# One decode step of attention with a gated block on one core: the gate moved to the start, one TensorE loop for all pairs, products moved to VectorE

## The chip, the core and the metric

The kernel runs on one core of a Trainium2 chip. The metric is the device time of one execution in microseconds. The kernel before took 687.77 us (median of three runs, 687.76 to 687.81). Lower is better.

## What is computed

```python
def reference(A_x, A_k_cache, A_v_cache, A_wq, A_wo, B_x, B_w_gate, B_w_up, B_w_down):
    x = A_x                                    # [1, 1, 512]
    xn = layernorm(x)                          # without scale and shift
    q = xn @ A_wq                              # 512 x 4096: 32 heads of 128
    scores = q . k_cache * 128 ** -0.5         # caches: 32 heads x 8192 x 128, float32
    o = softmax(scores) . v_cache
    s = o.reshape(4096) @ A_wo                 # 4096 x 512
    h = sigmoid(xn @ w_gate) * (xn @ w_up)     # 512 x 1376 each
    g = silu(h @ w_down)                       # 1376 x 512
    return x + s * g
```

Everything is float32. The two caches hold 134 MB each, wq and wo 8.4 MB each, the three matrices of the gated block 2.8 MB each: each byte is read once.

## The kernel before

The 32 heads are taken as 16 **pairs**. A pair's keys are one transfer of 64 KB to each of the 128 partitions, that is 8.389 MB: 64 partitions for a head, 128 positions of 128 numbers in each. Its values are another one. SBUF holds three such **slots**: keys of even and odd pairs alternate between slots 0 and 1, slot 2 holds values. All loads of consequence are issued by SP (SyncE) into one queue, in the order in which SP's program names them; SP stands still at a wait, and what it issues behind the wait comes later.

Work of pair i:

- VectorE (`scores`, L279 to L284): the whole key block times the query in place (L281), a sum over each position's 128 products (L282), and each partition's maximum (L284). With its last sum done, the slot is free for the keys of pair i+2.
- TensorE (`pair`, L244 to L262), a loop with the waits on semaphores written out: turns the maxima into a row (L246), VectorE takes the maximum of each head (`all_max`, L276), TensorE spreads it over the partitions (L248), ScalarE makes the exponentials with their sums (`powers_of`, L294 and L296), TensorE adds the sums (L250) and multiplies weights and values (L255, 32 groups of two instructions, into `po`). Then slot 2 is free for the next values. ScalarE copies `po` (`parts`, L301), and TensorE picks each head's part out of it (L260).
- VectorE (`heads_out`, L288 and L289) divides by the sum, and ScalarE's queue issues two small transfers for a pair that put the heads into `o_all` in the order that wo needs (`place`, L304 to L308).

15 pairs run in a TensorE loop (L264) whose first instruction has a fixed place in a block of code (`head_slot`); the last pair is written out behind it, with its values in slot 0, since they need not wait for slot 2.

At the **start**, SP issues wq (into slot 2), K0 and K1. TensorE multiplies the normalised x with wq (L206), ScalarE copies the query row, TensorE broadcasts it over the partitions (L218) and ScalarE copies it to `q_all` (L225). V0 is issued when wq has been used.

At the **end**, SP issues behind V15: w_gate, w_up, w_down into slot 2 once V14 has been used, and wo in six pieces (`W_ENDS`, of 14, 10, 4, 2, 1, 1 rows for each partition) into slot 1 once the last scores are done. TensorE computes gate, up (L356) and down (L384), with the sigmoid on ScalarE and transposes on VectorE (L366), and multiplies `o_all` with wo: rows 0 to 27 in four groups of partitions (L402), which are then copied and folded into `acc` (L371, L377), rows 28 to 31 directly into `acc` (L406). VectorE multiplies by the gate (L416), adds x (L418), and SP stores 2 KB (L422).

Of the kernel before, what the change touches and what calls it, by code (L numbers as in the profile page):

```python
# [9 lines left out]
AF = mybir.ActivationFunctionType  # L10
# [3 lines left out]
P = 128  # L14
EPS = 1e-5


@with_exitstack
def kernel(
# [35 lines left out]
    FH = FW + GP  # L55
    assert FH <= QT and FL % GP == 0 and 2 * KT * F + FP * D <= SLOT

    W_ENDS, W_FOLD = (14, 24, 28, 30, 31, 32), 28

    PE, DVE, ACT, SP, POOL = nc.tensor, nc.vector, nc.scalar, nc.sync, nc.gpsimd  # L60
# [15 lines left out]
    x_col, xc, sq, xn = (sb(n, KT) for n in ("x_col", "xc", "sq", "xn"))  # L76
    st, eps_t = sb("st", 8), sb("eps_t", 1)
    mx, nb, rs, rl = sb("mx", 4), sb("nb", 2), sb("rs", 1), sb("rl", 1)
# [9 lines left out]
    q_row = q_all[:, NP * Dh - NQ // NG * QT:].rearrange("p (b q) -> p b q", q=QT)  # L88
    wd_last = q_all[:, :D]
    sg, hg, s_tmp = (q_all[:, a:a + n] for a, n in ((D, FH), (D + FH, FH), (D + 2 * FH, QT)))  # L90
    assert D + 2 * FH + QT <= NP * Dh and FH <= QT

    weights = sb("weights", NB // HT, 2 * HT)
    sc = [sb(f"sc{i}", NB) for i in range(2)]
    on = [sb(f"on{i}", Dh) for i in range(2)]
    o1 = sb("o1", QT)
    hid = o1[:, :(FP + 1) * GP].rearrange("p (c i) -> p c i", i=GP)
# [4 lines left out]
    acc, po = bank("acc", P, GC), bank("po", P, QT)  # L102

    pn = bank("pn", 2, Dh + 1)
    pt, pm = bank("pt", P, P), bank("pm", P, 2)
# [36 lines left out]
    s_val = semaphore("s_val")  # L142
# [4 lines left out]
    ld_wq = load(SP, "wq", wq_t, wq.rearrange("(p k) c -> p k c", k=KT))  # L147
# [7 lines left out]
    def load_keys(i, *after):  # L155
        ld_k[i] = load(SP, f"k{i % 2}", slots[i % 2], rows_of(k_cache, i), *after)

    def load_values(i, *after):

        wait(SP, *after)  # L160
        SP.dma_start(slots[2], rows_of(v_cache, i)).then_inc(s_val, 16)

    load_keys(0)
    load_keys(1)
    ld_x = load(ACT, "x", x_col, xv.rearrange("(p k) -> p k", k=KT))


    c_ones = dve(DVE.memset(ones, 1.0))
    c_xrow = dve(DVE.memset(x_row, 0.0))
    ld_xr = load(ACT, "xr", x_row[0:P:GP, :], xv.rearrange("(g c) -> g c", g=NG), c_xrow)  # L170
    c_eps = dve(DVE.memset(eps_t, EPS))
# [4 lines left out]
    c_big = [dve(DVE.memset(t, 0.0)) for t in big]  # L176


    wait(DVE, ld_x)
# [21 lines left out]
    wait(PE, c_xn, c_big[-1], ld_wq)  # L201
    for k in range(KT):
        for b in range(NQ // NG):
            for g in range(NG):
                c = (b * NG + g) * QT
                ins = PE.matmul(big[b][g * GP:g * GP + 1, :], xn[:, k:k + 1], wq_t[:, k, c:c + QT],  # L206
                                start=(k == 0), stop=(k == KT - 1))
            if k == KT - 1:
                wq_done = pe(ins)
                wait(ACT, wq_done)  # L210
                c_row = act(ACT.copy(q_row[:, b, :], big[b]))
    load_values(0, wq_done)

    spreads, copies = {}, {}
    for t in range(NQ):
        b, g = divmod(t, NG)
        wait(PE, c_row if t == 0 else None, copies.get(t - 2))
        spreads[t] = pe(PE.matmul(big[t % 2], ones[g * GP:g * GP + 1, :], q_row[g * GP:g * GP + 1, b, :],  # L218
                                  start=True, stop=True))

        for u in (t,) if t < NQ - 2 else (NQ - 2, NQ - 1) if t == NQ - 1 else ():
            wait(ACT, spreads[t])
            q = big[u % 2].rearrange("p (i e d) -> p i e d", e=2, d=Dh)
            for e, h in enumerate(HALF):
                copies[u] = act(ACT.copy(qb[h, 2 * u:2 * u + 2, :], q[h, :, e, :]))  # L225
# [232 lines left out]
```

## Time and profile before

| | |
|---|---|
| median of the runs | 687.77 us |
| span of the profiled execution, first to last instruction | 685.6 us |
| VectorE busy | 574.0 us, 84% |
| TensorE busy | 222.1 us, 32% |
| ScalarE busy | 40.9 us, 6% |
| transfers | 293.84 MB, 429 GB/s over the span |
| instructions | 3694 |

The profile shows one execution. In a line of the time line stand the start and the length in microseconds, the engine, the line of the kernel, the operation, what it writes and reads with shapes, and in brackets the idle time before and what ended it. PE is TensorE's matmul, PEld its weight load, DVE VectorE, ACT ScalarE, POOL GpSimd, SPq and ACTq the queues of SyncE and ScalarE when they issue transfers. A group has its busy time and the mean length of one instruction in ns, then the idle time ahead of it.

### The profile page before, as it was taken

The numbers are of one execution on the slowest core, as the hardware profiler recorded it, in microseconds if no ns is written. First come the engines' busy times: TensorE is split into PE (matmuls) and PEld (weight loads), VectorE is DVE, ScalarE is ACT, GpSimd is POOL, SyncE is SP. The second block draws the span as 40 slices with busy tenths as digits, with TensorE's granted clock in tenths as the row PEclk, the third lists the DMA queues.
The fourth block names the chain that finished last, engine by engine and source line by source line (L and its number), as shares of the span: only waits on it lengthen the run. The fifth ranks groups of instructions, "written<-read, shape, count | busy, mean of one in ns | idle before, by whom it ended". The sixth has DMA issues, their size and how long they took to land.

```text
span 685.6 us, 3694 instructions
## 1 busy us (share of the span) xinstructions
PE 222.1 (32%) x1570; PEld 62.7 (9%) x1570; DVE 574.0 (84%) x136; ACT 40.9 (6%) x122; POOL 0.7 (0%) x6
## 2 busy tenths in 40 slices
PE   0550230605041140505042140506042140605656
PEld 0110000101010010101001010101000010101121
DVE  0159999999999999989898989989898989989220
ACT  0040100000000000000001010000001010000010
POOL 0000000000000000000000000000000000000000
PEclk9965575757566575757557575756657575756798
DMA  9999999999999999999999999999999999999996
GB/s 375 440 445 451 428 428 428 432 428 428 428 436 444 448 440 428 428 428 436 428 428 428 440 444 451 428 432 428 432 432 428 428 440 436 451 436 428 405 434 285
DMA packets 6614, 293.84 MB, mean 429 GB/s; under 512 B 1096, under 2 KB 1104, under 8 KB 1616
## 3 DMA queue, kind: packets, MB, share of 16 engines
q1 hardware_dynamic: 6200, 293.74, 99.1%
q10 hardware_dynamic: 408, 0.02, 0.0%
q8 instruction: 4, 0.07, 0.0%
q14 instruction: 2, 0.02, 0.0%
HBM read 293.74 MB, written 0.00 MB: 428 GB/s over the span
## 4 chain that ended last, share of the span: by engine, by line
DMA 37%; DVE 30%; PE 0%; SPq 0%; issue 0%
DMA slot<-in_A_k_cache_dram 31%; DVE slot L281 15%; DVE sc L282 15%; DMA slot<-in_A_wo_dram 6%; PE acc L406 0%; SPq L131 0%; PE pt L246 0%; PE acc L377 0%; DVE g_row L416 0%; DVE g_row L418 0%; DVE mx L276 0%
## 5 line engine op out<-in xcount | busy, mean ns | idle before, releaser
L281 DVE TENSOR_TENSOR slot<-slot,q_all 128x16384 f32<-128x16384 f32 x16 | 275.5, 17217 | 38.8 <-DMA slot<-in_A_k_cache_dram 38.8
L282 DVE TENSOR_REDUCE sc<-slot 128x128 f32<-128x16384 f32 x16 | 275.5, 17220 | 0.6
L255 PE MATMUL po<-slot,weights 128*8 128x512 f32 x1024 | 146.7, 737 | 232.1 <-PEq L242 231.5
L255 PEld LDWEIGHTS po<-slot,weights 128*8 128x8 f32 x1024 | 30.3, 103 | 335.3 <-issue 334.6
L246 PE MATMUL pt<-ident,mx 128*1 128x128 f32 x32 | 8.8, 374 | 148.6 <-PEq L242 148.6
L301 ACT COPY o<-po 128x512 f32<-128x512 f32 x16 | 9.4, 586 | 385.2 <-PE po L255 385.2
L260 PE MATMUL pn<-o,pick 128*2 128x128 f32 x128 | 16.5, 272 | 12.8 <-PEq L242 12.8
L180 DVE TENSOR_REDUCE st<-x_col 128x1 f32<-128x4 f32 x1 | 0.2, 157 | 20.7 <-DMA x_col<-in_A_x_dram 20.7
L246 PEld LDWEIGHTS pt<-ident,mx 128*1 128x1 f32 x32 | 1.8, 80 | 154.1 <-issue 154.1
L288 DVE RECIPROCAL rl<-pn 2x1 f32<-2x1 f32 x16 | 2.3, 146 | 14.6 <-PE pn L260 14.6
L294 ACT ACTIVATE nb<-pm 128x2 f32<-128x2 f32 x16 | 2.8, 173 | 190.4 <-PE pm L248 190.4
L416 DVE TENSOR_TENSOR g_row<-g_row,acc 128x128 f32<-128x128 f32 x1 | 0.3, 289 | 15.3 <-PE acc L406 15.3
L296 ACT ACTIVATE weights<-sc,nb 64x128 f32<-64x128 f32 x32 | 12.8, 399 | 0.9
L260 PEld LDWEIGHTS pn<-o,pick 128*2 128x2 f32 x128 | 9.9, 84 | 29.6 <-issue 27.2
L248 PE MATMUL pm<-mx,ones 1*128 1x2 f32 x32 | 8.8, 344 | 7.4 <-PEq L242 7.4
L402 PE MATMUL big<-slot,o_all 128*1 128x512 f32 x56 | 9.4, 765 | 4.8 <-DMA slot<-in_A_wo_dram 4.8
L250 PE MATMUL pn<-rs,half 128*2 128x1 f32 x32 | 3.0, 163 | 23.5 <-PEq L242 23.5
L218 PE MATMUL big<-q_all,ones 1*128 1x512 f32 x16 | 8.8, 850 | 1.6 <-ACT q_all L225 0.8
L206 PE MATMUL big<-slot,xn 128*1 128x512 f32 x64 | 9.0, 726 | 0.8 <-DVE xn L198 0.8
L248 PEld LDWEIGHTS pm<-mx,ones 1*128 1x128 f32 x32 | 7.9, 306 | 14.4 <-issue 14.4
L276 DVE TENSOR_REDUCE mx<-pt 1x2 f32<-1x128 f32 x16 | 4.5, 278 | 5.2 <-PE pt L246 5.0
L182 PE MATMUL pt<-st,ones 128*128 128x1 f32 x2 | 0.6, 362 | 23.4 <-DVE st L180 23.4
(61 smaller groups left out, 62.1 us busy)
## 6 DMA issues: line engine op xcount, KB each, us to landing
slot<-in_A_wo_dram SPq DMA_DIRECT2D x1, 3584.0 KB, 32.5
slot<-in_B_w_gate_dram SPq DMA_DIRECT2D x1, 2752.0 KB, 16.8
slot<-in_B_w_up_dram SPq DMA_DIRECT2D x1, 2752.0 KB, 22.8
slot<-in_B_w_down_dram SPq DMA_DIRECT2D x1, 2560.0 KB, 27.3
slot<-in_A_wo_dram SPq DMA_DIRECT2D x1, 2560.0 KB, 38.2
slot<-in_A_wo_dram SPq DMA_DIRECT2D x1, 1024.0 KB, 40.2
o_all<-on ACTq DMA_DIRECT2D x32, 0.5 KB
slot<-in_A_wo_dram SPq DMA_DIRECT2D x1, 512.0 KB, 40.9
```

Source lines behind the costliest of these rows:

```text
L206: ins = PE.matmul(big[b][g * GP:g * GP + 1, :], xn[:, k:k + 1], wq_t[:, k, c:c + QT], start=(k == 0), stop=(k == KT - 1))
L218: spreads[t] = pe(PE.matmul(big[t % 2], ones[g * GP:g * GP + 1, :], q_row[g * GP:g * GP + 1, b, :], start=True, stop=True))
L246: PE.matmul(pt[0:1, :], mx[:, 0:1], ident, start=True, stop=True).then_inc(turned, 1)
L248: PE.matmul(pm, ones[:1, :], mx[:1, 1:3], start=True, stop=True).then_inc(spread_m, 1)
L255: ins = PE.matmul(po[g * GP:g * GP + 2 * HT, :], weights[:, j // HT, :], v[:, j * Dh:(j + HT) * Dh], start=(j < HT * NG), stop=(j >= NB - ...
L260: ins = PE.matmul(pn[:, :Dh], pick[:, b:2 * HT:HT], o1[:, b * Dh:(b + 1) * Dh], start=(b == 0), stop=(b == HT - 1))
L276: DVE.reduce_max(mx[:1, 1:3], pt[0:1, :].rearrange("o (e p) -> o e p", e=2), axis=AX.X).then_inc(reduced, 1)
L281: wait(DVE, dve(DVE.tensor_mul(k, k, qb[:, i:i + 1, :].to_broadcast([P, NB, Dh]))))
L282: summed[i] = dve(DVE.reduce_sum(sc[i % 2], k, axis=AX.X))
L296: ACT.activation(weights[h, :, e * HT:(e + 1) * HT], sc[i % 2][h].rearrange("p (g b) -> p g b", b=HT), AF.Exp, bias=nb[h, e:e + 1], scale= ...
L301: ACT.copy(o1, po).then_inc(copied, 1)
L402: ins = PE.matmul(big[0][g:g + 1, :], o_all[:, r:r + 1], wo_t[:, r, :], start=(r < NG), stop=(r + NG >= W_FOLD))
```

## The change

Five things change together.

1. **The gated block goes to the start.** SP issues wq in two halves, w_gate and w_up (into slot 0), K0 (now slot 1), then w_down (slot 2) when the last query broadcast is done, K1 (slot 0) when the up product is done, and V0 (slot 2) when the whole gate is done.
2. **Products move to VectorE.** Query, gate and up are made in place on VectorE: the matrix's rows k of each partition are multiplied by that partition's x and summed over k (`in_place`, four instructions; for wq the last is cut into eight pieces), and TensorE sums over the partitions with a matrix of ones, which also broadcasts. Of wo's 32 rows, 0 to 15 are made on VectorE with two partial sums in turn, 16 to 29 on TensorE as before, 30 and 31 directly into `acc`.
3. **One TensorE loop for all 16 pairs**, V15 in slot 2 as well. `head_slot` goes. The loads at the end are cut: V14, V15 and K15 each into 84 and 44 of 128 blocks, in the order K15's first cut, V14, K15's second cut, V15 (which waits until V14 is used), wo (into slot 1, once K14's scores are done). TensorE's part is recorded while the other engines' parts are written, and played at the end.
4. **The heads are divided together at the end.** `heads_out` is one transpose for each pair from PSUM to PSUM; the sums are kept in `den`. Behind the last pair come one reciprocal, one product over all heads, and four transposes into `o_all`. The `place` transfers go.
5. **Hints.** Everything behind the first loads stands in a body with a branch back that is never taken; the branches of TensorE, ScalarE and VectorE carry a hint, placed at the body's start (TensorE: at the loop's start).

x is loaded once (`x_row`) and turned by VectorE; before, it was loaded a second time into a column of all partitions.

```diff
-    W_ENDS, W_FOLD = (14, 24, 28, 30, 31, 32), 28
+    W_ENDS, W_DVE, W_FOLD = (14, 24, 28, 30, 31, 32), 16, 30
+    V_CUT, K_CUT = 84, 84
...
-    ld_wq = load(SP, "wq", wq_t, wq.rearrange("(p k) c -> p k c", k=KT))
+    ld_wq = [load(SP, f"wq{n}", wq_t[:, n:n + 2, :], wq_v[:, n:n + 2, :]) for n in (0, 2)]
+    ld_g = load(SP, "wg", wg_t, w_gate.rearrange("(p k) f -> p k f", k=KT))
+    ld_u = load(SP, "wu", wu_t, w_up.rearrange("(p k) f -> p k f", k=KT))
...
+    load_keys(0, FULL)
+    once = nc.alloc_registers("once")
+    nc.regs_mov(once, 0)
+    nc.br("body")
+    body.enter_context(nc.body("body"))
+    hints = {e: e.mark_branch_hint_location() for e in (ACT, DVE)}
...
+    def in_place(w, k, cols=slice(None)):
+        y = w[:, 0, cols]
+        if k == 0:
+            return dve(DVE.tensor_scalar(y, y, xn[:, 0:1], None, op0=ALU.mult))
+        return dve(DVE.scalar_tensor_tensor(y, w[:, k, cols], xn[:, k:k + 1], y, op0=ALU.mult, op1=ALU.add))
+    for k in range(KT - 1):
+        wait(DVE, ld_wq[k // 2], t if k else None)
+        t = in_place(wq_t, k)
...
     for t in range(NQ):
+        wait(PE, in_place(wq_t, KT - 1, c), copies.get(t - 2))
+        spreads[t] = pe(PE.matmul(big[t % 2], ones, wq_t[:, 0, c], start=True, stop=True))
...
+    load(SP, "wd", wd_t, w_down[:FP * P, :].rearrange("(p r) e -> p r e", r=FP), spreads[NQ - 1])
+    ld_d = load(SP, "wd", wd_last, w_down[F - FL:, :].rearrange("(p r) e -> p r e", r=FC))
...
+    load_keys(1, FULL, rows[1])
...
+    gated = column_sums(big[1], s_gate)
+    load_values(0, FULL, gated)
...
-    with nc.Fori(0, NP - 1, engines=OrderedEngineSet([PE.engine]), head_slot={PE.engine: 0}):
-        pair(slots[2], lambda: taken(s_val, 16))
-    pair(slots[NP % 2], lambda: PE.wait_ge(v_last, 16))
+    pair(slots[2])
+    each = PE.take()
...
-        wait(DVE, dve(DVE.reciprocal(rl[:2], pn[:, Dh:])), placed.get(i - 2))
-        outs[i] = dve(DVE.tensor_scalar(on[i % 2][:2], pn[:, :Dh], rl[:2], None, op0=ALU.mult))
+        o = o_t[:, 2 * WP * i:2 * WP * i + Dh].rearrange("r (e a) -> r a e", a=WP)
+        turned_out[i] = dve(DVE.transpose(o, pn.rearrange("e (a r) -> e a r", r=WR)))
...
         if i >= 2:
-            load_keys(i, summed[i - 2])
-            load_values(i - 1, (valued, i - 1))
+            tail = i == NP - 1
+            load_keys(i, K_LAST[:1] if tail else FULL, summed[i - 2])
+            load_values(i - 1, V_LAST if tail else FULL, (valued, i - 1))
+            if tail:
+                load_keys(i, K_LAST[1:])
+                load_values(i, V_LAST, (valued, i))
...
+    t = dve(DVE.reciprocal(den[:GP], den[:GP]))
     heads_out(NP - 1)
+    wait(DVE, dve(DVE.tensor_mul(heads, heads, den[:GP].unsqueeze(2).to_broadcast([GP, H, WP]))))
+    for g in range(NG):
+        rows = slice(g * GP, (g + 1) * GP)
+        placed = dve(DVE.transpose(o_all[rows, :], o_t[:, rows]))
...
     def to_fold(after):
-        wait(ACT, after)
-        return act(ACT.copy(s_tmp, big[0]))
+        wait(DVE, after, t_part)
+        return dve(DVE.tensor_add(s_tmp, part[0], big[0]))
...
+        for r in range(r0, min(r1, W_DVE)):
+            n = r % 2
+            wait(DVE, ld if r == r0 else None, t_parts[n])
+            if r < 2:
+                ins = DVE.tensor_scalar(part[n], wo_t[:, r, :], col, None, op0=ALU.mult)
+            else:
+                ins = DVE.scalar_tensor_tensor(part[n], wo_t[:, r, :], col, part[n], op0=ALU.mult, op1=ALU.add)
+            t_parts[n] = dve(ins)
+    t_part = dve(DVE.tensor_add(part[0], part[0], part[1]))
...
+    PE.play(before)
+    with nc.Fori(0, NP, engines=pe_only):
+        hints[PE.engine] = PE.engine.mark_branch_hint_location()
+        PE.play(each)
+    PE.play(after)
...
+    nc.regs_alu(once, once, 1, op=ALU.add)
+    for e in (ACT, DVE, PE.engine, POOL, SP):
+        br = e.br_lt(once, 1, on_true="body", on_false="done")
+        if e in hints:
+            br.branch_hint(hints[e])
```

More of the change, by code (lines that the diff above doesn't have):

```diff
@@ L228 @@
[L228 to L237 removed]
+        c = slice(t * QT, (t + 1) * QT)
+        wait(PE, in_place(wq_t, KT - 1, c), copies.get(t - 2))
@@ new lines @@
+    wait(DVE, t, rows[1])
+    for d, c in zip(sums[1], chunks):
+        t = dve(DVE.tensor_mul(hg[:, c], sg[:, c], d[:, :c.stop - c.start]))
+    wait(DVE, t)
+    for d in (big[0], po, acc):
+        dve(DVE.memset(d, 0.0))
+    for g in range(NG):
+        r = slice(g * GP, (g + 1) * GP)
+        dve(DVE.transpose(hid[r, :FP, :], hg[r, g * FW:(g + 1) * FW].rearrange("p (i c) -> p c i", c=FP)))
+    t = dve(DVE.transpose(hid[:GP, FP:, :], hg[:GP, NG * FW:].rearrange("p (i c) -> p c i", c=FC)))
@@ L414 @@
         r0 = r1
[L415 removed]
+    wait(DVE, pe(ins), c_gate)
     t = dve(DVE.tensor_mul(g_row, g_row, acc))
```

275 lines of the change are left out of this document (147 added, 128 removed).

## The prediction

> **What bounds the kernel now.** I read the page's slices first, then the groups by form, then the time line of the last quarter.
>
> ```profile
> GB/s 375 440 445 451 428 428 428 432 428 428 428 436 444 448 440 428 428 428 436 428 428 428 440 444 451 428 432 428 432 432 428 428 440 436 451 436 428 405 434 285
> HBM read 293.74 MB, written 0.00 MB: 428 GB/s over the span
> L281 DVE TENSOR_TENSOR slot<-slot,q_all 128x16384 f32<-128x16384 f32 x16 | 275.5, 17217 | 38.8 <-DMA slot<-in_A_k_cache_dram 38.8
> L282 DVE TENSOR_REDUCE sc<-slot 128x128 f32<-128x16384 f32 x16 | 275.5, 17220 | 0.6
> ```
>
> The transfers never pause: every slice but the last is near the mean. VectorE, at 84%, only waits for keys. Starts of the score product give the rate:
>
> ```profile
> 42.28 17.23 DVE L281 TENSOR_TENSOR slot<-slot,q_all 128x16384 f32<-128x16384 f32 x1 [13.93 <-DMA slot<-in_A_k_cache_dram]
> ...
> 294.47 17.23 DVE L281 TENSOR_TENSOR slot<-slot,q_all 128x16384 f32<-128x16384 f32 x1 [1.83 <-DMA slot<-in_A_k_cache_dram]
> ...
> 603.74 17.23 DVE L281 TENSOR_TENSOR slot<-slot,q_all 128x16384 f32<-128x16384 f32 x1 [3.02 <-DMA slot<-in_A_k_cache_dram]
> ```
>
> All three start as a key block lands (pairs 0, 7 and 15). From pair 7 to 15 there are 16 transfers of 8.389 MB (128 x 16384 x 4 bytes) in 309.27 us: **19.33 us each, 434 GB/s**. From pair 0 to 7 there are 13 in 252.19 us, 19.40 each: some 0.9 us was lost once. The end follows the last bytes of `wo`:
>
> ```profile
> 680.54 0.62 PE L406 MATMUL acc<-slot,o_all 128*1 128x128 f32 x16
> 681.16 0.40 PE L377 MATMUL acc<-q_all,ones 128*1 128x128 f32 x8
> 681.82 0.10 PEld L406 LDWEIGHTS acc<-slot,o_all 128*1 128x1 f32 x8 [0.34 <-DMA slot<-in_A_wo_dram]
> 682.28 0.29 DVE L416 TENSOR_TENSOR g_row<-g_row,acc 128x128 f32<-128x128 f32 x1 [15.32 <-PE acc L406]
> 682.92 0.64 SPq L422 DMA_DIRECT2D out_dram<-g_row  x1
> ```
>
> The last piece lands at 681.77, row 31 takes 0.46, and from L416 to the end of the span (685.57) are 3.29 us. The median of the runs, 687.77, is 2.2 us over this span; I keep that distance.
>
> **The change, part by part.** *Bytes.* The same matrices, except that w_down's last rows shrink from 256 KB (128 rows) to 192 KB (96 rows): 65 KB, 0.15 us. [...] So by the transfers alone the last piece lands at 681.77 - 0.35 = 681.4, if nothing pauses and nothing on the engines is later.
>
> *Start: does the queue run dry?* Order now: wq in two halves, gate, up (5.636 MB, 13.0 us), K0, then w_down behind the last query broadcast, K1 behind the up product, V0 behind the whole gate.
>
> ```profile
> slot<-in_A_wq_dram SPq DMA_DIRECT2D x1, 22.0
> q10 hardware_dynamic: 408, 0.02, 0.0%
> 23.14 0.16 DVE L180 TENSOR_REDUCE st<-x_col 128x1 f32<-128x4 f32 x1 [20.65 <-DMA x_col<-in_A_x_dram]
> 37.96 7.74 PE L218 MATMUL big<-q_all,ones 1*128 1x512 f32 x12 [0.84 <-ACT q_all L225]
> 662.46 2.31 PE L384 MATMUL big<-slot,o 128*1 128x512 f32 x18 [2.68 <-DVE o L367]
> 670.91 5.81 PE L402 MATMUL big<-slot,o_all 128*1 128x512 f32 x28 [4.61 <-DMA slot<-in_A_wo_dram]
> L284 DVE TENSOR_REDUCE mx<-sc 128x1 f32<-128x128 f32 x16 | 4.6, 286 | 0.5
> ```
>
> wq (issued at 0.96) lands at 23.0, gate and up at 36.0, K0 at 55.3, w_down at 61.8, K1 at 81.1, V0 at 100.4. VectorE's price: from 128 elements (0.286 us) to 16384 (17.22) an element costs 1.042 ns and an instruction 0.153. A product of 4096 is then 4.42 us, one of 1376 1.59, one of 512 0.69. Products k = 0 and 1 lie under the second half of wq, even if x came as late as the 23.14 of before (then two of 4.42 are added below). k = 2 ends at 27.4, the eight pieces of k = 3 at 32.9, gate's four at 39.2, up's four at 45.6. The broadcasts, 1.29 each (7.74 for six), end at 38. So w_down is issued at 38 (17 us ahead of K0's landing), K1 at 45.6 + six instructions of 0.6 = 49 (13 ahead of w_down's; 4 if x came late), V0 at 61.8 + 26 instructions of 0.13 (2.31/18) to 0.21 us (5.81/28, a slower clock) + 1.5 = 67 to 69 (12 ahead of K1's). K0's scores start at 56 instead of 42 and end at 90.5, ten ahead of V0's landing, when K2 must be queued. All hidden; a pause would cost its own length at the end.
>
> *Middle.* Nothing in the period changes but two small instructions in `heads_out` for one transpose, under VectorE's waits (1.83 and 3.02 above).
>
> *Tail.* Before, 16.9 MB of gate weights and wo followed V15; now only wo does, 8.39 MB. The cover behind the last scores halves. Before, up to K15's landing, 31 slot-sized transfers had come (wq, 16 K, 14 V); now K14 has 29 in front with 8.454 MB of gate matrices: 251.73 against 260.05 MB, 19.17 us less, so **K14 lands at 603.72 - 19.17 = 584.55**. From there VectorE never waits:
>
> ```profile
> 112.55 0.29 DVE L284 TENSOR_REDUCE mx<-sc 128x1 f32<-128x128 f32 x1
> 112.75 0.14 DVE L288 RECIPROCAL rl<-pn 2x1 f32<-2x1 f32 x1
> ...
> 113.81 17.20 DVE L281 TENSOR_TENSOR slot<-slot,q_all 128x16384 f32<-128x16384 f32 x1
> ...
> 584.53 9.78 PE L255 MATMUL po<-slot,weights 128*8 128x512 f32 x64 [20.00 <-PEq L242]
> 594.37 0.33 SPq L161 DMA_DIRECT2D slot<-in_A_v_cache_dram  x1
> ...
> 638.25 0.28 DVE L284 TENSOR_REDUCE mx<-sc 128x1 f32<-128x128 f32 x1
> 641.67 0.19 PE L250 MATMUL pn<-rs,half 128*2 128x1 f32 x2 [1.39 <-PEq L242]
> 642.44 9.84 PE L255 MATMUL po<-slot,weights 128*8 128x512 f32 x64 [0.57 <-DMA slot<-in_A_v_cache_dram]
> 654.15 0.15 DVE L288 RECIPROCAL rl<-pn 2x1 f32<-2x1 f32 x1 [14.56 <-PE pn L260]
> ```
>
> K14's two passes with gaps, 34.49, and 1.26 from its reduction's end to the next product (112.55 to 113.81): K15's first 84 blocks start at 620.30, the two passes over both cuts take 34.5 + 0.3 for two more instructions, to **655.1** (K15's second cut lands at 642.5, when VectorE is still on the first, to 643.0). Maximum to the end of L250: 3.65, so the V15 product starts at 658.8 (its first cut lands at 655.2), 9.84 long, to 668.6; 1.87 more until the heads are there (652.28 to 654.15): 670.5.
>
> ```profile
> 1.47 1.02 DVE L176 MEMSET big<- 128x512 f32 x2
> L176 DVE MEMSET big<- 128x512 f32 x2 | 1.0, 485 | 0.2
> 660.99 1.27 DVE L366 STREAM_TRANSPOSE o<-q_all 128x32 f32<-128x32 f32 x10
> L366 DVE STREAM_TRANSPOSE o<-q_all 128x32 f32<-128x32 f32 x10 | 1.3, 197 | 0.0
> L392 DVE TENSOR_TENSOR g_row<-g_row,big 128x128 f32<-128x128 f32 x1 | 0.3, 287 | 0.2 <-ACT g_row L390 0.2
> L363 DVE TENSOR_TENSOR q_all<-q_all,big 128x352 f32<-128x352 f32 x1 | 0.5, 507 | 0.0
> ```
>
> Dividing all heads at the end: one transpose of 128 columns (0.2 to 0.5), one product like L392 (0.29), four transposes (four at 0.12, one behind the other, or at 0.2): 1.3, `placed` at 671.8. Then 16 products of 512 columns, an operation the trace lacks. Lower bound 0.535 from start to start, as the two memsets of 512 (1.02 - 0.485); upper 0.69, a whole instruction. I take **0.60**, since L288 starts 0.20 after L284 whose 128 elements are 0.133 by the slope, so 0.07 over the slope; the two partial sums alternate, so no product waits for the one just before it. 16 x 0.60 + 0.09 = 9.7, to 681.5. Sum of the partial sums 0.69, sum with PE's rows (like L363, with 512) 0.67, gaps 0.04: 682.9. Fold 0.40 and row 31 with its semaphores 0.3: 683.6. The rest 3.29: span 686.9, less 0.2 for `place`: **686.7, and with 2.2, 688.9**. PE's 14 rows lie under VectorE's 16: PE has them at 680.7, just behind the 30th row's landing near 680.1.
>
> [...]
>
> *Costed at nothing:* one TensorE loop with the last pair inside, since TensorE waits for VectorE's maximum anyway; a branch into the body, under the first transfer. V14's issue has little cover: V13 lands at 603.9, its product takes 9.9, so 613.8; K15's first cut lands at 616.6. An issue to an empty queue needs about 2.7 us ahead (23.0 - 0.96 - 19.33), so 0.1 is left, where the old period had 9.5; a miss costs up to 1 us.
>
> **The rivals.** (a) *The transfers still set the end*: VectorE is through before 680.8. For it: only 1.5 to 2 us are missing, and bounds of 0.535 in the products and 0.2 less in the transposes give 1.3 of them. Time: 681.4 + 3.8 + 2.2 = 687.4; with the loss of 0.9 avoided as well, 686.4.
>
> ```profile
> DMA packets 65, 4.21 MB, mean 421 GB/s; under 512 B 0, under 2 KB 0, under 8 KB 0
> q8 instruction: 1, 0.02, 0.6%
> ...
> q8 instruction: 4, 0.07, 0.0%
> ```
>
> The first two rows are for 45 to 55 us: one fetch of instructions as TensorE entered its loop, within the stretch in which the 0.9 us went; the last, of the page, counts four in all. [...]
>
> (c) *The product-and-add costs two passes* (1.07 + 0.15 for 512 columns): the tail's grows by 14 x 0.6 = 8.4, to 697. L281, two sources at 1.05 ns an element, speaks against it. (d) *The change doesn't do what it says*: if K1 or V0 is late, the gate at the start costs what it saved, as a pause: 2 to 6 us, 691 to 695. The covers worked out above speak against it.
>
> **How the numbers follow.** Forecast, VectorE's tail sets the end: 0.50, its own range 687.5 to 690.5. (a) 0.26, (b) 0.13, (c) 0.05, (d) 0.06. The measurement tells 0.2%, 1.4 us, from no change: limits 686.4 and 689.1. Of the forecast 0.31 lies within and 0.19 above; of (a) half each within and below; the others above. Faster 0.13, same 0.44, slower 0.43. The range goes from 686.0, under which transfers leave no room, to 694, which takes in the small forms of (b) and (d).
>
> **What would show it.** Right: VectorE without a wait from K14's landing (near 584.6) to the end, products 0.6 apart, the last of them at 681 to 682, and the final L416's counterpart waiting for the fold, not for wo. Wrong: a gap in the GB/s row at 36 to 100 us (d); more instruction fetches than four and slots over 19.4 us (b); wo's last piece landing after VectorE's sum (a); products over 0.7 apart (c).

## The result, and the profile after

The changed kernel takes **689.08 us** (median of 12 runs, 688.52 to 691.23), the kernel before on the same chip 687.39 us: ratio 1.0026, 95% interval 1.0018 to 1.0035. The change costs about 0.25%. One execution of one variant below (mix12) took 815.49 us, where its other eleven took 687.84 to 689.75; it is a slow run and in none of the numbers.

Two executions of the changed kernel were profiled, and they differ: the first has a time of 690.75 us, the second 687.99. Spans, transfer rates and instruction fetches on their pages:

```profile
span 688.8 us, 3331 instructions
GB/s 373 434 434 453 441 426 426 426 426 426 426 483 430 426 426 426 426 426 453 460 426 426 426 426 426 426 472 441 426 426 426 426 426 426 466 417 426 414 421 231
```

```profile
span 686.2 us, 3331 instructions
GB/s 371 430 445 409 447 466 432 428 428 428 428 428 428 436 447 462 428 428 428 428 428 428 428 436 470 439 428 428 428 428 428 428 428 447 466 405 419 438 425 274
q8 instruction: 1, 0.02, 0.0%
```

Every slice but the last is again near the mean, so the new start lets nothing run dry. Of the six instruction fetches before (four of 16 KB in q8, two of 8 KB in q14) one of 16 KB is left, at the very end (685.56) in the second profile and behind the last instruction (690.01) in the first. (Times of single packets are on the time line's clock, which starts with the first instruction; where an expectation below says 106 or 105.7 for a fetch, this clock has 105.6 and 105.3.) The start, from the first profile's time line:

```profile
13.06 2.35 DVE L268 TENSOR_SCALAR slot<-slot,xn 128x4096 f32<-128x4096 f32 x1 [1.50 <-DMA slot<-in_A_wq_dram]
15.52 4.49 DVE L269 SCALAR_TENSOR_TENSOR slot<-slot,xn 128x4096 f32<-128x4096 f32 x1
...
37.80 0.80 SPq L164 DMA_DIRECT2D slot<-in_B_w_down_dram  x2
48.84 0.34 SPq L164 DMA_DIRECT2D slot<-in_A_k_cache_dram  x1
55.15 17.23 DVE L383 TENSOR_TENSOR slot<-slot,q_all 128x16384 f32<-128x16384 f32 x1
68.94 0.33 SPq L208 DMA_DIRECT2D slot<-in_A_v_cache_dram  x1
```

w_down, K1 and V0 are issued at 37.8, 48.8 and 68.9 (38, 49 and 67 to 69 were forecast), and the scores of pair 0 begin at 55.15 (56).

The end in the second profile, from K14's landing on:

```profile
583.87 17.23 DVE L383 TENSOR_TENSOR slot<-slot,q_all 128x16384 f32<-128x16384 f32 x1 [2.80 <-DMA slot<-in_A_k_cache_dram]
...
612.19 0.80 SPq L208 DMA_DIRECT2D slot<-in_A_v_cache_dram  x2
...
619.65 11.34 DVE L383 TENSOR_TENSOR slot<-slot,q_all 128x10752 f32<-128x10752 f32 x1
...
638.53 0.80 SPq L208 DMA_DIRECT2D slot<-in_A_v_cache_dram  x2
...
654.39 0.29 DVE L386 TENSOR_REDUCE mx<-sc 128x1 f32<-128x128 f32 x1
...
657.97 8.80 PE L37 MATMUL po<-slot,weights 128*8 128x512 f32 x64
...
668.64 0.32 DVE L391 STREAM_TRANSPOSE wide<-pn 32x128 f32<-32x128 f32 x1 [10.03 <-PE pn L37]
...
669.39 0.92 DVE L436 STREAM_TRANSPOSE o_all<-wide 32x32 f32<-32x32 f32 x4
670.42 0.88 DVE L466 TENSOR_SCALAR q_all<-slot,o_all 128x512 f32<-128x512 f32 x2
671.21 9.36 DVE L468 SCALAR_TENSOR_TENSOR q_all<-slot,o_all,q_all 128x512 f32<-128x512 f32 x14
675.92 4.49 PE L37 MATMUL big<-slot,o_all 128*1 128x512 f32 x26 [7.32 <-DMA slot<-in_A_wo_dram]
...
680.68 0.69 DVE L472 TENSOR_TENSOR q_all<-q_all 128x512 f32<-128x512 f32 x1
681.47 0.69 DVE L448 TENSOR_TENSOR q_all<-q_all,big 128x512 f32<-128x512 f32 x1
...
682.90 0.29 DVE L497 TENSOR_TENSOR g_row<-g_row,wide 128x128 f32<-128x128 f32 x1 [0.74 <-PE wide L37]
```

(L37 is the line that plays TensorE's recorded part; the tiles tell which part it is.) From L466 to L472 VectorE goes without a wait, and the sum with TensorE's rows (L448) follows with no bracket: TensorE had them. **VectorE's products set the end**, as forecast. The last packet of wo, in the trace's packets, ends at 680.46; the product with the gate starts 2.44 later. Before, the last packet ended at 681.44 and that product started at 682.28, 0.84 later. So the transfers end 1.0 earlier and what follows them is 1.6 longer: +0.6, which is the difference of the spans (686.2 to 685.6).

The same stretch in the first profile:

```profile
612.81 0.80 SPq L208 DMA_DIRECT2D slot<-in_A_v_cache_dram  x2
...
638.91 0.81 SPq L208 DMA_DIRECT2D slot<-in_A_v_cache_dram  x2
...
677.61 6.03 PE L37 MATMUL big<-slot,o_all 128*1 128x512 f32 x26 [8.13 <-DMA slot<-in_A_wo_dram]
681.71 0.69 DVE L472 TENSOR_TENSOR q_all<-q_all 128x512 f32<-128x512 f32 x1
...
684.12 0.69 DVE L448 TENSOR_TENSOR q_all<-q_all,big 128x512 f32<-128x512 f32 x1 [1.72 <-PE big L37]
...
685.55 0.29 DVE L497 TENSOR_TENSOR g_row<-g_row,wide 128x128 f32<-128x128 f32 x1 [0.74 <-PE wide L37]
```

V14 and V15 are issued 0.6 and 0.4 us later than in the second, and that was too late: by the trace's packets the first cuts of their transfers end 13.57 and 13.63 after the transfer ahead of them, against 12.69 in the second profile: two pauses of 0.88 and 0.94. The last packet of wo ends at 682.14. And here VectorE waits 1.72 us for TensorE (L448's bracket), whose 26 products took 6.03 instead of 4.49. The granted clock says why; a window's columns are its length, TensorE's busy time (with its instructions), granted clock, DMA share and GB/s, the first profile ahead of the second:

```profile
679.00:683.00 4.00, 4.00 (x26) 0.50 0.56 220
```

```profile
679.00:683.00 4.00, 2.67 (x40) 1.00 0.32 122
```

In the trace's clock records TensorE is at half clock from 671.8 to 678.6 in the second profile, and from 673.2 to 683.4 in the first. So the tail has two lanes, VectorE's 16 rows and TensorE's 14. In the second profile they end within a microsecond of each other, and TensorE's clock decides which of them ends last. The two profiles are of executions with spans of 686.2 and 688.8; most executions have 686.7 to 687.3, and none of those was profiled, so which lane ends last in them is not shown.

### The profile page after: what moved, and what is told of

Its sections match the earlier page's. It is cut to its first block, busy times and chain, and to the rows that moved or that the text cites. A ratio compares the mean times of both kernels' runs of the same rounds, so it can differ in the third digit from the quotient of the medians.

```text
span 688.8 us, 3331 instructions
## 1 busy us (share of the span) xinstructions
PE 215.1 (31%) x1366; PEld 62.0 (9%) x1366; DVE 614.6 (89%) x155; ACT 42.5 (6%) x137; POOL 1.2 (0%) x10
## 5 line engine op out<-in xcount | busy, mean ns | idle before, releaser
L383 DVE TENSOR_TENSOR slot<-slot,q_all 128x16384 f32<-128x16384 f32 (+2 forms) x17 | 275.7, 16215 | 27.5 <-DMA slot<-in_A_k_cache_dram 27.5
L384 DVE TENSOR_REDUCE sc<-slot 128x128 f32<-128x16384 f32 (+2 forms) x17 | 275.7, 16216 | 0.6
L37 PE MATMUL po<-slot,weights 128*8 128x512 f32 x1024 | 146.2, 731 | 252.1 <-PEq L37 252.0
L37 PEld LDWEIGHTS po<-slot,weights 128*8 128x8 f32 x1024 | 30.3, 103 | 354.4 <-issue 354.4
L37 PE MATMUL wide<-ident,mx 128*1 128x128 f32 x32 | 9.4, 395 | 120.1 <-PEq L37 120.1
L269 DVE SCALAR_TENSOR_TENSOR slot<-slot,xn 128x512 f32<-128x512 f32 (+2 forms) x16 | 24.3, 1552 | 3.0 <-DMA slot<-in_A_wq_dram 2.6
L37 PE MATMUL pn<-o,pick 128*2 128x128 f32 x128 | 16.5, 272 | 12.8 <-PEq L37 12.8
L37 PE MATMUL big<-slot,ones 128*128 128x512 f32 (+1 forms) x28 | 12.6, 600 | 22.3 <-DVE slot L269 20.4
L391 DVE STREAM_TRANSPOSE wide<-pn 32x128 f32<-32x128 f32 x16 | 5.0, 309 | 10.5 <-PE pn L37 10.5
L37 PEld LDWEIGHTS wide<-ident,mx 128*1 128x1 f32 x32 | 1.8, 80 | 124.3 <-issue 124.3
L37 PEld LDWEIGHTS pn<-o,pick 128*2 128x2 f32 x128 | 9.9, 84 | 29.6 <-issue 27.2
L375 DVE TENSOR_REDUCE mx<-wide 1x2 f32<-1x128 f32 x16 | 4.5, 279 | 8.7 <-PE wide L37 8.7
L37 PE MATMUL pm<-half,rs 128*32 128x2 f32 x32 | 3.8, 189 | 23.6 <-PEq L37 23.6
L37 PE MATMUL pm<-mx,ones 1*128 1x2 f32 x32 | 8.8, 343 | 7.4 <-PEq L37 7.4
L37 PE MATMUL big<-slot,o 128*1 128x512 f32 (+1 forms) x26 | 5.2, 834 | 13.8 <-DMA slot<-in_B_w_down_dram 13.8
L468 DVE SCALAR_TENSOR_TENSOR q_all<-slot,o_all,q_all 128x512 f32<-128x512 f32 x14 | 9.4, 743 | 0.0
L37 PEld LDWEIGHTS pm<-mx,ones 1*128 1x128 f32 x32 | 7.9, 305 | 14.9 <-issue 14.9
L37 PE MATMUL big<-slot,o_all 128*1 128x512 f32 x28 | 6.5, 1011 | 8.1 <-DMA slot<-in_A_wo_dram 8.1
L285 ACT COPY q_all<-big 64x256 f32<-64x256 f32 x16 | 5.9, 367 | 21.6 <-PE big L37 21.1
```

The lines of the kernel that those rows point to most:

```text
L37: ins = getattr(self.engine, name)(*args, **kwargs)
L269: return dve(DVE.scalar_tensor_tensor(y, w[:, k, cols], xn[:, k:k + 1], y, op0=ALU.mult, op1=ALU.add))
L285: copies[t] = act(ACT.copy(qb[h, 2 * t:2 * t + 2, :], q[h, :, e, :]))
L375: DVE.reduce_max(mx[:1, 1:3], pt[0:1, :].rearrange("o (e p) -> o e p", e=2), axis=AX.X).then_inc(reduced, 1)
L383: wait(DVE, dve(DVE.tensor_mul(k[:, j, :], k[:, j, :], qb[:, i:i + 1, :].to_broadcast([P, n, Dh]))))
L384: summed[i] = dve(DVE.reduce_sum(sc[i % 2][:, j], k[:, j, :], axis=AX.X))
```

## The experiments

All times are medians; beside each group of variants the kernel before ran on the same chip (687.4 to 687.6 each time). The ratios compare with that one.

**The changed kernel again.**

> The changed kernel as it is, for a second profile beside the variants. Its first profile fell in an execution with a span of 688.8 us where most others have 687.1. Both theories: about 689.0 us, 1.6 over the kernel before. Theory 1 (PE's late rows): TensorE's first product with wo starts when wo's second piece lands (677.5 in the first profile), 26 instructions at 0.21 us, and VectorE's sum waits for it. Theory 2 (the forecast: VectorE's products set the end): VectorE's sum starts when its own products are through, with no wait for TensorE.

Measured: 688.89 us (687.99 to 691.51, 9 runs), ratio 1.0028 (1.0018 to 1.0038). Its profile is the second one above: theory 2's picture, where the first profile was theory 1's. The spans of the nine executions are 686.2 to 689.7, a spread that the kernel before, with 685.4 to 686.1 beside them, does not have.

**Fewer rows on VectorE.** Two edits of one number:

```diff
-    W_ENDS, W_DVE, W_FOLD = (14, 24, 28, 30, 31, 32), 16, 30
+    W_ENDS, W_DVE, W_FOLD = (14, 24, 28, 30, 31, 32), 14, 30    # w14
+    W_ENDS, W_DVE, W_FOLD = (14, 24, 28, 30, 31, 32), 2, 30     # w2
```

> Two rows of wo (14 and 15) go from VectorE to TensorE. Theory 1 (TensorE's rows behind wo's second piece set the end, at a slow clock): four more instructions of 0.21 us: 0.9 us slower than the changed kernel, about 689.9. Theory 2 (VectorE's 16 products set the end): two products of 0.6 us fewer: 1.2 us faster, about 687.8.

> VectorE keeps only rows 0 and 1 of wo; TensorE takes 2 to 29. Theory 1: TensorE begins with wo's first piece at 671.5 instead of the second at 677.5, and has a fast clock (0.11 us for an instruction, as in the kernel before) when the second lands: the fold comes 2.4 us earlier, about 686.7. Theory 2 with the transfers as the next limit: 1.7 to 2.5 faster as well. If TensorE stays at 0.21 us for an instruction: 28 rows take 12 us from 671.5 on, and the time stays at 689.

With 14 rows: 688.54 us, ratio 1.0018 (1.0009 to 1.0027), 0.35 under the changed kernel by the medians, with overlapping intervals: neither 0.9 slower nor 1.2 faster. Its time line is from an execution of 689.78 us; the fastest of the eleven takes 687.58:

```profile
676.85 6.33 PE L37 MATMUL big<-slot,o_all 128*1 128x512 f32 x32 [8.00 <-DMA slot<-in_A_wo_dram]
679.62 0.69 DVE L472 TENSOR_TENSOR q_all<-q_all 128x512 f32<-128x512 f32 x1
...
683.26 0.69 DVE L448 TENSOR_TENSOR q_all<-q_all,big 128x512 f32<-128x512 f32 x1 [2.95 <-PE big L37]
```

VectorE has its sum 1.06 earlier than in the second profile (two rows of 0.663, less 0.27 by which it starts later), and then waits 2.95 for TensorE, whose 32 products take 6.33. With 2 rows: 689.78 us, ratio 1.0032 (1.0022 to 1.0043), slower than any of its cases had it:

```profile
585.61 17.23 DVE L383 TENSOR_TENSOR slot<-slot,q_all 128x16384 f32<-128x16384 f32 x1 [2.81 <-DMA slot<-in_A_k_cache_dram]
...
678.30 4.71 PE L37 MATMUL big<-slot,o_all 128*1 128x512 f32 x32 [1.67 <-DMA slot<-in_A_wo_dram]
683.06 0.69 DVE L448 TENSOR_TENSOR q_all<-q_all,big 128x512 f32<-128x512 f32 x1 [9.17 <-PE big L37]
...
684.49 0.29 DVE L497 TENSOR_TENSOR g_row<-g_row,wide 128x128 f32<-128x128 f32 x1 [0.74 <-PE wide L37]
```

Here the product with the gate starts 1.58 behind the last packet of wo (682.91) instead of 2.44: the tail is 0.9 shorter. But K14 lands 1.7 later, and the time is worse. The edit did a second thing: TensorE's program grew, and its trace has an instruction fetch at 105.6. The runs on code, below, take that up. They also show that the last packet itself ends later where there is a fetch (681.97 in mix8 with one, 680.53 in best2 and 680.42 in mix10 without). That the shorter tail comes from the other split is therefore not shown by this run alone.

**The first piece of wo 3.6 us later, with no pause.** Rows 24 to 29 of wo are issued ahead of V15, as cover:

```diff
+                wait(SP, summed[NP - 2])
+                for n in (2, 3):
+                    early[n] = load_wo(n)
...
+    ld_o = [early[n] if n in early else load_wo(n) for n in range(len(W_ENDS))]
```

> Rows 24 to 29 of wo (1.57 MB, 3.6 us) are issued before V15, to cover V15's issue, which waits for the product with V14. Nothing else is changed. Theory 1 (a pause of 0 to 0.9 us at V15 because its issue comes too late): no pause at V15 in the profile, the slow executions go, median 0.3 to 0.9 lower, 688.0 to 688.6. If V15's later landing (3.6 us) reaches TensorE's product: no gain.

Measured: 691.44 us, ratio 1.0061 (1.0048 to 1.0074).

```profile
673.44 0.88 DVE L472 TENSOR_SCALAR q_all<-slot,o_all 128x512 f32<-128x512 f32 x2 [2.10 <-DMA slot<-in_A_wo_dram]
...
684.69 0.69 DVE L454 TENSOR_TENSOR q_all<-q_all,big 128x512 f32<-128x512 f32 x1 [0.30 <-PE big L37]
...
686.12 0.29 DVE L503 TENSOR_TENSOR g_row<-g_row,wide 128x128 f32<-128x128 f32 x1 [0.74 <-PE wide L37]
```

There is no pause at V15, and the last packet of wo ends at 680.45, as in the second profile. But VectorE's first product starts 3.0 later (673.44 against 670.42), for want of wo's first rows, and the end is 3.2 later (686.12 against 682.90). The same bytes end at the same moment and the kernel, meant to gain 0.3 to 0.9, is over 2 us slower: **this shows that the work behind wo's first pieces sets the end, not the transfers.** It does not show that it is VectorE's share of it: both lanes start later, VectorE is through with its own sum at 684.39, and the next one still waits 0.30 for TensorE's rows (L454's bracket).

**K15's first cut longer**, so that V14 has more cover:

```diff
-    V_CUT, K_CUT = 84, 84
+    V_CUT, K_CUT = 84, 108
```

> K15's cut moves from 84 to 108 of 128 blocks. Theory 1 (the queue runs dry because V14 and V15 are issued too late: K15's first cut covers V14's issue, its second cut covers V15's): V14's pause of 0.9 us goes, V15's cover shrinks by 3.6 us and its pause grows by as much; the last bytes land 2.7 us later, about 691.7. Theory 3 (the cut transfers are slower in themselves, because of their smaller packets): no pause moves, and the time stays within 0.3 us.

Measured: 691.17 us, ratio 1.0055 (1.0042 to 1.0069).

```profile
641.97 0.80 SPq L208 DMA_DIRECT2D slot<-in_A_v_cache_dram  x2
...
672.59 0.88 DVE L466 TENSOR_SCALAR q_all<-slot,o_all 128x512 f32<-128x512 f32 x2 [1.53 <-DMA slot<-in_A_wo_dram]
```

V14, issued at 612.94, has no pause any more (at 612.81 with the shorter cut it had one of 0.88). V15 is issued at 641.97, 3.4 later than in the second profile, with less of K15 queued ahead, and the queue runs dry for 2.6: wo's last packet ends at 683.27. The time is within 0.5 of theory 1's 691.7. So the pauses are a matter of how much lies ahead in the queue at the issue; small packets as such are not slow, since V14, cut as before, has no pause behind a longer cut, and in the second profile its first cut (5.51 MB in packets of 43 KB) takes 12.69, 434 GB/s, the rate that the prediction read from packets of 64 KB.

**The program's length.** 14 TensorE products of 128 columns, into a buffer that nobody reads, stand at the end of TensorE's program:

```diff
+    for _ in range(14):
+        PE.matmul(big[1][0:1, :GC], ones[:, 0:1], ident, start=True, stop=True)
```

> The changed kernel with 14 small products more at the very end of TensorE's program, behind the last one that anything waits for: as many instructions more as the kernel with two rows on VectorE had, which fetched code at 106 us and lost 1.3 us of the stream there. Theory 4 (TensorE's program, once longer than the blocks that it holds, is fetched during the stream, and each fetch delays one transfer engine and so all that follows): one fetch in the stream, the last bytes 1 to 1.3 us later, 690.0 to 690.3. Theory 5 (that loss came from the other split of wo's rows or by chance): no fetch, 689.0.

Measured: 691.34 us, ratio 1.0061 (1.0048 to 1.0074). The queues in the window from 105 to 107 us, and the landing of K14:

```profile
q8 instruction: 1, 0.02, 3.2%
```

```profile
585.22 17.23 DVE L383 TENSOR_TENSOR slot<-slot,q_all 128x16384 f32<-128x16384 f32 x1 [2.81 <-DMA slot<-in_A_k_cache_dram]
```

The added products run at 685, when everything is over, and yet K14 lands **1.35 later** (585.22 against 583.87): TensorE's program, 14 products longer, now brings 16 KB of code at 105.2, in the loop. By the packets, the transfer then under way ends 20.64 after the one ahead of it, and those behind it 19.32. From there on one of the 16 transfer engines is 1.3 behind: it ends its last packet of 64 KB at 604.17 and the others by 602.85. By its delay of 1.3, against 1.0 for the fetch (3.2% of 16 engines in 2 us), it is taken to be the one that serves the fetch; a key block's last packet is this engine's, so each later landing waits for it. That TensorE holds its program in blocks, as theory 4 has it, no trace shows; the fetch and the delay are what the run shows. The rest, in this profile, is in V15's product: it starts at 659.11, 1.1 later than in the second profile, and takes 9.96 instead of 8.80, so VectorE begins with wo's rows 2.3 later (672.72). All five executions take 690.90 or more, above the 690.0 to 690.3 that theory 4 had; why the other four do is not shown.

**Without the hints.**

```diff
-    hints = {e: e.mark_branch_hint_location() for e in (ACT, DVE)}
+    hints = {}
-        hints[PE.engine] = PE.engine.mark_branch_hint_location()
```

> The three branch hints are left out. [...] Theory 4 (TensorE's whole program is short enough to stay): no fetch, 688.9.

Measured: 690.74 us, ratio 1.0046 (1.0033 to 1.0059). From the page:

```profile
q8 instruction: 1, 0.02, 0.0%
q14 instruction: 2, 0.02, 0.0%
```

Three fetches (8 KB at 59.8, 16 KB at 107.6, 8 KB at 156.1), K14 at 585.15, 1.3 later; at the last keys three of the 16 transfer engines are behind the others, by 1.3, 0.9 and 0.6. The hints are worth 1.8 us here by the medians and 1.2 by the ratios (1.0046 against 1.0028), whose intervals overlap; the landing, 1.3 later, is the firmer figure. But the loop's 15 jumps back bring no 15 fetches: without the hints, too, three fetches are made in all and not one for each pass.

**Several remedies together.** K15's cut at 92, rows 24 to 29 of wo ahead of V15 and first on TensorE, so that it starts when VectorE does, and wo's other rows in pieces that fit the split. The split: 14 rows on VectorE (best2, shown), 12 (mix12), 10 (mix10), 8 (mix8).

```diff
-    W_ENDS, W_DVE, W_FOLD = (14, 24, 28, 30, 31, 32), 16, 30
-    V_CUT, K_CUT = 84, 84
+    W_ENDS, W_DVE, W_FOLD = (6, 14, 20, 24, 30, 31, 32), 14, 30
+    V_CUT, K_CUT = 84, 92
...
+                wait(SP, summed[NP - 2])
+                for n in (4,):
+                    early[n] = load_wo(n)
...
+    order = [n for n in [4, 0, 1, 2, 3] if spans[n][1] > W_DVE]
```

> All together: K15 cut at 92 (V14's issue covered by 1.2 us more), rows 24 to 29 of wo ahead of V15, TensorE begins with these as soon as the heads are in place, wo's first 24 rows in four pieces, VectorE keeps 14 rows. Expected: no pause, last bytes at 680.7, VectorE's sum at 680.3, TensorE's rows at 680.5 to 681.5, 687.0 to 687.8, about the kernel before. If TensorE falls back to its slow clock between the pieces: 688.

> As the version with all together, but VectorE keeps 8 rows and TensorE takes rows 8 to 29 (24 to 29 first, then 8 to 13 as they land, so that it stays busy from 671.4 to 676 and has its fast clock when the last pieces come). TensorE's program is 32 instructions longer than in the changed kernel, 24 shorter than where code was fetched at 106 us. If no code is fetched: TensorE's rows at 680.2, VectorE's last sum at 680.9, the end as early as the transfers allow: 686.8, 0.7 below the kernel before. If code is fetched in the stream: 1 to 1.3 later, 688.

> The same with 12 rows on VectorE (to 679 for its own sum) and rows 12 to 29 on TensorE, 16 instructions longer than the changed kernel. TensorE has less to do between 673 and 676.8 and may fall to its slow clock: 687.2 to 688.

> As best2 with 10 rows on VectorE; TensorE's program has 104 products, between 12 rows (102) and 8 rows (106, a fetch at 105.7 us). If the length of the program decides whether code is fetched, this narrows the point: without a fetch 687.2 to 688.4, with one 688.7 or more and one transfer engine about 1.3 us behind the others at the last keys.

Measured: best2 688.36 us, ratio 1.0016 (1.0007 to 1.0024); mix12 688.38, 1.0016 (1.0007 to 1.0025); mix8 688.7, 1.0022 (1.0012 to 1.0031); mix10 690.75, 1.0045 (1.0031 to 1.0059). None reaches the time hoped for it; best2 and mix8 are within 0.7 of what was expected for a slow clock and for a fetch (688 both). In the profiles of best2, mix8 and mix10 nothing pauses at V14 or V15. best2's time line and its clock:

```profile
671.42 1.88 PE L37 MATMUL big<-slot,o_all 128*1 128x512 f32 x12 [1.76 <-DVE o_all L446]
...
677.14 4.43 PE L37 MATMUL big<-slot,o_all 128*1 128x512 f32 x18 [3.84 <-DMA slot<-in_A_wo_dram]
...
682.48 0.69 DVE L454 TENSOR_TENSOR q_all<-q_all,big 128x512 f32<-128x512 f32 x1 [1.37 <-PE big L37]
```

```profile
676.00:680.00 4.00, 2.86 (x14) 0.54 (x18) 4.00 (x7) 0.00 (x0) 0.00 (x0) 0.50 0.98 403
```

TensorE starts early (671.42, at 0.157 a product), then waits 3.84 us for wo's next rows, and meets them at clock 0.50 (third number from the end; the busy times of the five engines stand ahead of it). The early start does not keep the clock up over the pause, and with 14 rows on VectorE it is TensorE's rows that the last sum waits for, 1.37 us, in an execution without a pause. mix8 has a fetch at 105.3 and K14 at 585.35, as the padded kernel; best2 and mix10, with 100 and 104 products in TensorE's program outside of the loop where mix8 has 106 and the padded kernel 112, have none there, and K14 at 583.92 and 583.79. So for these kernels the point lies between 104 and 106 products.

mix10 missed both expectations: nothing is fetched in the stream, the spans of four of its five executions are 685.3 to 685.5, *shorter* than the kernel before's (685.5 to 686.0 beside it), and yet it takes 690.75. The time lies **outside the span**: 5.0 to 5.5 us between span and time, where the kernel before has 1.7 to 1.8 in all its executions. Behind the last instruction the trace has one thing, in the window from 686.2 to 692 us:

```profile
q8 instruction: 1, 0.02, 1.5%
```

a fetch of 16 KB at 687.37, which takes 1.44. A fetch behind the end is in the first profile of the changed kernel, too (690.01, 0.93 long), where span and time are only 1.9 apart. The other variants have 1.8 to 2.2 in most executions and up to 3.5 in single ones; mix12 and fold31 (below), at 102 products, have 2.0 to 3.5 and 2.0 to 2.7. So it is not settled why mix10's 3.4 us more are spent.

**The fold ahead of the last row.** As best2 with 9 rows on VectorE, row 30 with the others, and the fold before row 31, so that one row alone follows the last landing:

```diff
-    W_ENDS, W_DVE, W_FOLD = (6, 14, 20, 24, 30, 31, 32), 14, 30
+    W_ENDS, W_DVE, W_FOLD = (9, 14, 20, 24, 30, 31, 32), 9, 31
...
-    order = [n for n in [4, 0, 1, 2, 3] if spans[n][1] > W_DVE]
+    order = [n for n in [4, 0, 1, 2, 3, 5] if spans[n][1] > W_DVE]
```

> Rows 0 to 8 of wo on VectorE, all others on TensorE, those of the early piece first; the fold stands ahead of row 31, which is the last piece. Theory (two limits compete in the tail, VectorE's products and TensorE's rows, which begin late at a slow clock): with VectorE's part shortened to 9 rows and TensorE's 12 rows more under way before the last pieces land, the last bytes set the end: the final product with the gate starts 1.2 us behind wo's last landing, about 682.1 in an execution without pauses, span 685.4, time 687.2 (ratio 0.9995 to 1.0005). TensorE's program has 102 products as with 12 rows on VectorE, so no code fetch in the stream is expected. Rival (TensorE's rows at half clock set the end whatever the split): 688.4 to 688.7, as with 14, 12 and 8 rows, and TensorE is what the final sums wait for.

Measured: 688.43 us (688.21 to 689.40, 11 runs), ratio 1.0015 (1.0006 to 1.0024).

```profile
677.58 0.69 DVE L478 TENSOR_TENSOR q_all<-q_all 128x512 f32<-128x512 f32 x1
...
679.65 1.89 PE L37 MATMUL big<-slot,o_all 128*1 128x512 f32 x10 [0.56 <-DMA slot<-in_A_wo_dram]
...
681.58 0.69 DVE L454 TENSOR_TENSOR q_all<-q_all,big 128x512 f32<-128x512 f32 x1 [3.31 <-PE big L37]
...
683.01 0.29 DVE L500 TENSOR_TENSOR g_row<-g_row,wide 128x128 f32<-128x128 f32 x1 [0.74 <-PE wide L37]
```

The theory did not hold. The rival's time and its wait did (L454's bracket, 3.31 for TensorE), but not its reason: TensorE has its full clock from 664.3 to 684.8 in the clock records. VectorE is through at 678.3, the last packet of wo ends at 680.57, and still the product with the gate starts 2.44 later. What sets the end now is the series behind wo's late pieces: rows 20 to 23 land at 679.6, row 30 at 680.2, ten products take 1.89, the sum on VectorE 0.7, the fold and row 31 another 0.7. The kernel before, with four rows directly into `acc` and its fold between them, has 0.84 there. This version varies least (ten of eleven within 0.5 us) and is about 0.5 better than the changed kernel by the medians, but it does not beat the kernel before, nor does any other that was run.

All of them side by side; the last packet of wo, the start of the product with the gate, and the distance are from each kernel's profiled execution, mix12's excepted:

| kernel | K14 product starts | last packet of wo | product with the gate | distance | median us |
|---|---|---|---|---|---|
| before | (other order) | 681.44 | 682.28 | 0.84 | 687.4 to 687.6 |
| changed, first profile | 583.74 | 682.14 | 685.55 | 3.41 | 689.08 |
| changed, second profile | 583.87 | 680.46 | 682.90 | 2.44 | 688.89 |
| 14 rows | 584.01 | 681.40 | 684.69 | 3.29 | 688.54 |
| 2 rows (fetch) | 585.61 | 682.91 | 684.49 | 1.58 | 689.78 |
| wo's rows 24 to 29 early | 583.87 | 680.45 | 686.12 | 5.67 | 691.44 |
| K15 cut at 108 | 584.07 | 683.27 | 686.08 | 2.81 | 691.17 |
| padded (fetch) | 585.22 | 682.08 | 685.21 | 3.13 | 691.34 |
| no hints (fetches) | 585.15 | 683.03 | 685.62 | 2.59 | 690.74 |
| best2 | 583.92 | 680.53 | 683.91 | 3.38 | 688.36 |
| mix8 (fetch) | 585.35 | 681.97 | 683.60 | 1.63 | 688.70 |
| mix10 | 583.79 | 680.42 | 682.98 | 2.56 | 690.75 |
| fold31 | 583.93 | 680.57 | 683.01 | 2.44 | 688.43 |

The two with a short distance are the two that leave VectorE 2 or 8 rows and put the rest on TensorE; both have a longer program with a fetch, which moves the last packet back by more than the distance gains. The fetch is a rival explanation of the short distance, since it delays the packet from which the distance is counted: mix10 and fold31, with 10 and 9 rows on VectorE and no fetch in the stream, have 2.56 and 2.44, no less than the changed kernel's second profile.

## Why the prediction came out as it did

**The mechanism was right where nothing pauses and TensorE's clock comes up in time:** VectorE's tail sets the end, behind transfers that end a microsecond earlier than before. The second profile shows it. The kernel whose first piece of wo came late shows that the transfers do not set the end, but there TensorE's rows were the last by 0.30.

**The terms, against that profile.** K14 lands at 583.85, not 584.55: the forecast took 19.17 us off the landing of before and so carried along the 0.9 us that were lost at the fetch at 48.7; the new program has no fetch there. From K14 to K15's first cut 35.78 (35.75 forecast), both passes over K15 34.7 (34.8), maximum to V15's product 3.6 (3.65). V15's product took 8.80 (9.30 in the first profile), not 9.84, the length in the profile of before: it changes with the granted clock (9.84 at 0.71 and 9.21 at 0.76 before, 9.30 at 0.75 in the first profile; in the second the clock is 0.55 from 657 to 662 and 1.00 from 662 to 668), and one row was taken for a constant. Heads 1.87 behind it, as forecast. The division takes 1.78 (668.64 to 670.42), not 1.3: the last pair's transpose takes 0.32 and the four at the end 0.92. No run shows the 0.2 that the forecast takes off for `place` (and the sum of (a), within its 0.35): a transfer of 8.389 MB takes 19.328 on average before (29 of them from 62.2 to 622.7) and 19.319 in the second profile (27 from 81.2 to 602.8), 0.3 in all, but each `place` transfer has only eight data packets of 16 or 128 bytes, and that the 0.3 is theirs is not shown. The 16 products and their gaps take 10.26 (670.42 to 680.68), not 9.7: a product-and-add follows the one before it after 0.663, where 0.60 was taken between the bounds 0.535 and 0.69. Both lie within bounds, the upper one nearly reached. Sums and fold: 680.68 to 682.90, 2.2 (2.1). In all, -0.7 for K14, -1.0 for V15's product, +0.5 and +0.6 for division and products, and the rest nearly nothing: 682.9 for the product with the gate, where the forecast had 683.6 (683.4 less `place`).

The products overlap a little: 14 of 747 ns each take 9.36, so each starts 0.08 before the one ahead has ended. A whole instruction by the slope, 0.69, was nearer than the value taken.

**The step that did not hold in every execution** is the one sentence on TensorE: "PE's 14 rows lie under VectorE's 16: PE has them at 680.7". Rows 16 on are in wo's second piece, which lands at 675.9 to 677.6; TensorE has idled for seven to eight microseconds by then (its brackets), begins at half clock (until 678.6 in the second profile, until 683.4 in the first), and has its rows at 680.8 or at 684.1 (the end of its last two products, 680.24 and 0.59 in the second profile; L448's start in the first). The forecast took this lane's end from the landing of row 30 alone; it worked out neither its start nor its length at the slower of the two durations that it quoted (0.13 and 0.21 for a product); 28 products of 0.23, as in the first profile, from 677.6 come to 684.0. So the step is right for the second profile and 3.4 us too early for the first. The spread goes with the granted clock: from 679 to 683 it is 1.00 in the second profile and 0.50 in the first, with half-clock stretches of 6.83 and 10.24 us ahead of the rise. What sets the length of such a stretch is not shown.

**Cover.** "0.1 is left ... a miss costs up to 1 us" for V14's issue was right in kind and size: none at 612.19, 0.88 at 612.81. V15's issue, which waits until V14 is used, was not priced; it is as tight (none at 638.53, 0.94 at 638.91). V14's issue follows the product with V13, whose length differs (8.83 in the second profile; 9.59 in the first, at a granted clock of 0.73). The product with V14 is the shorter one in the first profile (9.46 against 9.78), but it starts 0.7 later, since V14 has paused: there the second pause follows from the first. That the median, 689.08, lies within 0.2 of the forecast is luck in part, made of two errors: the second profile's time, 687.99, is 0.9 under it (0.5 in the span, 0.4 in the distance from span to time, 1.8 and not 2.2), and the median is 1.1 over that execution, by pauses and slow clock as far as the two profiles tell, which stood in the forecast only as a possible miss. Set against the kernel before, the forecast was 1.1 us slower (688.9 to 687.77) and the measurement is 1.7 slower (689.08 to 687.39).

**The rivals.** (a) The transfers don't set the end: they end at 680.46, and the end moves with the landing of wo's first pieces while they stand still. Its gain of 0.9 at the fetch is real, though, and stood only there and not in the forecast. (b), that the loop's code is fetched again in each pass, does not occur: the program as changed has no fetch in the stream. What the runs show is smaller: a longer program or one without hints has one to three fetches, and K14 lands 1.3 us later. So no run shows the repeated fetch behind (b)'s 0.13. The cost of a single one is not hidden: one transfer engine is still 1.3 us behind the others at the last keys. (c) is out: 0.663 for a product-and-add of 512 columns. (d) is out: nothing at the start is late.

**Where the expected gain went.** Moved gate, shorter bytes and one fetch less bring the last packet of wo forward by 1.0 us. The work that covered the last pair's scores went to the start with the gate, and the 1.6 us between 0.84 and 2.44 are what is now uncovered behind wo; the median is another 1.1 us over this, by pauses and clock as far as the two profiles tell.

## What to carry to other kernels

When work that follows the last loads is moved to the start, the transfers get no shorter: it only leaves the tail uncovered (here the last packet of wo ended 1.0 us earlier and the product with the gate started 0.6 later), so price the last pair's chain and each engine that shares the last matrix separately, each at its slowest measured duration. An issue that waits for a TensorE product needs cover for the longest time measured of that product (here 8.5 to 10.0 us, by the profile). And the length of an engine's program can cost by itself (14 unused products more: a fetch in the stream, K14 1.35 us later): compare instruction fetches, and the distance between span and time, for each variant before its split is judged.

## What the runs showed of the hardware that was not expected

- A fetch of code (16 KB, 1.0 us) in the midst of the stream leaves one of the 16 transfer engines 1.3 us behind, and it does not catch up: K14 lands 1.3 to 1.7 later 480 us after the fetch, in all four variants that have one (of the 1.7, with 2 rows, 0.45 was lost ahead of the fetch). The kernel before has such a fetch, too, at 48.7: one engine ends its part of K1 at 62.23 and the others by 61.25.
- A product of 4096 columns with a scalar per partition took 2.35 us, a product-and-add of the same columns 4.49.
- The distance from span to time isn't a constant of the chip: 1.7 to 1.9 for the kernel before, 5.0 to 5.5 for mix10, with spans shorter than before's. A kernel cannot be ranked by its span alone.
